# Attention with routed rows on one core: wider table elements, an early block, and a reordered start and end

## The chip, the cores and the metric

The kernel runs on one NeuronCore of a Trainium2 chip. The metric is device time in microseconds (us) of one execution. Engines are named as in the profile: PE (TensorE, its weight loads PEld), DVE (VectorE), ACT (ScalarE), POOL (GpSimd) and SP (SyncE, which here only issues DMAs).

## What is computed

Sigmoid attention over 8 batches and 12 heads (448 tokens, head dimension 64), followed by a mixture-of-depths layer on the joined heads (448 rows of 768 per batch): the 128 rows with the highest gate score go through a two-layer MLP, and the result, weighted by the sigmoid of the score, is added to them.

```python
def _attn_ref(q, k, v):                       # 8 x 12 x 448 x 64, float32
    scale = 1.0 / np.sqrt(q.shape[-1])
    scores = scale * np.matmul(q, k.transpose(0, 1, 3, 2)) - np.log(S)
    attn = 1.0 / (1.0 + np.exp(-scores))
    return np.matmul(attn, v)

def _moe_ref(x, w_gate, w1, w2, capacity):    # x 8 x 448 x 768, w1 768 x 1024, capacity 128
    scores = np.einsum('bsd,d->bs', x, w_gate)
    out = x.copy()
    for b in range(B):
        top_idx = np.argpartition(-scores[b], capacity)[:capacity]
        xe = x[b, top_idx]
        h = np.maximum(xe @ w1, 0.0)
        ye = h @ w2
        g = 1.0 / (1.0 + np.exp(-scores[b, top_idx]))
        out[b, top_idx] = x[b, top_idx] + g[:, None] * ye
    return out
```

## The kernel before, in words

**Attention.** The 96 heads make 24 groups of 4 heads ("quads", three to a batch). A step `s` (12 of them) takes two quads, `x` 0 and 1, and goes through 7 slots `n`. A slot (s, n) holds 16 groups of score matmuls (`score`, L344; 32 x 64 tiles of the array, results in the two PSUM tiles `PA`), two sigmoids on ACT (`squash`, L358) and some of the value matmuls (`value`, L373). These lag: values of step s begin in slot (s, 4) and end in slot (s+1, 3), with NF = 3, and gather in the four PSUM banks `PO[x][pr]`. `rounds` gives the order of the value matmuls of a step; for steps in `LATE` (those from the first step with a block on) `first_slots`, `LOW`, `HIGH` and `last_slot` give another one, in which the banks of quad 0 are done earlier than those of quad 1. `join` writes one element into a bank with ACT (L382), which sets PE's later writes to this bank behind what came before; a `split` slot does it for both quads at once.

q and k are turned on DVE in 32 x 32 blocks (`turn`: L326 to L331 for k into a new tile, L318 for q in place, L321 for the first q by halves). Finished banks are taken out by DVE (`take`, L394) into `x_b` and stored in DRAM as rows of `out` (`store`, L411, packets of 128 bytes).

**Routing.** For each batch DVE forms the gate scores (`gate_part`, `gate`, L402 to L435), which go to DRAM (L430) and come back spread over all partitions (`spread`, L442). `rank` (L450, L453) counts for every token how many score higher. `place` (L457) makes an integer rank of it; then four indirect DMAs on POOL (L464, one for each of NC = 4 columns of tokens) write each token's pair (token, score) from `who`, 8 bytes, to the row of a DRAM table that is its rank, and four plain DMAs on POOL (L469) read the first 128 rows back. Each of the four tables holds only its own column's tokens, the rest being zero from `blank`, so that `fetch` (L485) gets the list by adding the four. Then `gather` (L506, indirect, POOL) fetches the chosen rows, 3 KB each. For the last two batches, 6 and 7, no table is used: DVE makes a 0/1 matrix `hot` (L473), and PE multiplies it with `who` (`choose`, L481).

**MLP.** Batches go in pairs through a scheme of seven products for a 2 x 2 block matrix in each layer: `turn_rows` transposes the gathered rows on PE (L524), `first` (L560) and `second` (L624) are the products of both layers, `first_sums` and `second_sums` their combinations on DVE and ACT. For batches 0 to 5 this work is cut into `BLOCKS`, placed in slot (s, 3) of steps 5 to 11, after the scores of that slot; so the block of step s falls between the ends of slots (s, 3) and (s, 4). What is left (batches 6 and 7, and a part of batches 4 and 5's) is done in `rest` after the last slot.

**Order.** Nothing is scheduled by a planner: the program order is the order of each engine and of each DMA queue. Loads of q, k, weights and the stores are issued by SP, the v loads by SP up to step 5 and by ACT after it; all DMAs of the routing but one are issued by POOL. `after(s, n)` says what follows slot (s, n) on DVE, POOL and SP. Two small lists in it matter here: `RANKED`, the slots of the ranking, and `FETCHED`, those of `fetch`:

```python
RANKED = [(3, 1), None, (6, 1), None, (9, 1), None, (11, 6)]
FETCHED = {(4, 1): 0, (5, 6): 1, (6, 5): 2, (8, 4): 3, (9, 5): 4, (11, 3): 5}
```

Tiles of a pool of one buffer take the place of the last tile of that name: `rows_t` holds early loads of k and v and later the turned rows, `hidden` two early sigmoids and later the hidden layer, and `raw_v` the v of a step.

Of the kernel before, what the change touches and what calls it, by code (L numbers as in the profile page):

```python
# [9 lines left out]
F32 = mybir.dt.float32  # L10
# [7 lines left out]
def kernel(  # L18
# [11 lines left out]
    nc = tc.nc  # L30

    B, H, S, Dh = q.shape
# [98 lines left out]
    NA = NU - 2  # L131

    def load_v(s):


        if s >= NS:
            return
        if s in (1, 3):
            t = moe.tile([P, 6 * KH * P], F32, name="rows_t")[:, :4 * NU * Dh]
        else:  # L140
            t = vals.tile([P, 4 * NU * Dh], F32, name="raw_v")
        raw_v[s] = t = t.rearrange("p (h c) -> p h c", h=4)

        def block(x, r, n):
            return bass.AP(tensor=v.tensor,
                           offset=v.offset + (8 * s + 4 * x) * S * Dh + r * Dh,
                           ap=[[TB * Dh, TT], [S * Dh, 4], [1, n * Dh]])
# [114 lines left out]

    who = [const.tile([P, NC, 2], F32, name=f"who{x}") for x in range(2)]
    tables = [dram.tile([(B - 2) * S, 2], F32, name=f"table{c}", bufs=1) for c in range(NC)]
    slots = const.tile([P, CAP], F32, name="slots")
# [5 lines left out]
    def blank(zero):  # L271

        for t in tables:
            nc.sync.dma_start(out=t.rearrange("(b s) x -> b (s x)", s=S)[:, :2 * CAP],
                              in_=zero[:B - 2, :2 * CAP])

# [32 lines left out]
    def turn(which, *quads):  # L309


        for i in quads:
            if i >= NQ:
                return
            t = heads[which, i].rearrange("p (r e d) -> p e r d", e=2, d=TT)
            if which == "q":
                if i:
                    nc.vector.transpose(heads["q", i], heads["q", i])  # L318
                else:
                    for e in range(2):  # L320
                        nc.vector.transpose(t[:, e], t[:, e])  # L321
                continue
            heads["k", i] = kt = head.tile([P, 2, TB, TT], F32, name="kT")
            for e in range(2):
                if i > 1:
                    nc.vector.transpose(kt[:, e], t[:, e].rearrange("p (a n) d -> p n a d", a=2))  # L326
                else:
                    nc.vector.transpose(
                        kt[:, e, :2 * NA],
                        t[:, e, :2 * NA].rearrange("p (a n) d -> p n a d", a=2))  # L330
                    nc.vector.transpose(  # L331
                        kt[:, e, 2 * NA:],
                        t[:, e, 2 * NA:].rearrange("p (a n) d -> p n a d", a=2))

    def score(s, n, e, pr, out):

        for y in range(2):
            x, c, step = chunks(s, n, y)
            r = 2 * column(s, n, y)
            kt = heads["k", 2 * s + x]  # L340
            qt = heads["q", 2 * s + x].rearrange("p (r e t) -> p e r t", e=2, t=TT)
            for h in range(2 * pr, 2 * pr + 2):
                d = slice(h * TT, (h + 1) * TT)
                nc.tensor.matmul(  # L344
                    out[y * Dh:(y + 1) * Dh, h % 2, :S],
                    kt[d, e, r:r + 2].rearrange("d r t -> d (r t)"), qt[d, e],
                    start=(e == 0), stop=(e == 1))
# [30 lines left out]

    def join(x):

        for t in PO[x]:
            nc.scalar.activation(t[Dh:Dh + 1, S:S + 1], bias_s[Dh:Dh + 1], AF.Copy)  # L382

# [33 lines left out]
    def gate(b):  # L417
# [11 lines left out]
        scores = dram.tile([TB, TT], F32, name="scores")  # L429
        nc.gpsimd.dma_start(out=scores, in_=total[:TB])  # L430
        by_token = moe.tile([TT, TT], F32, name="by_token")
# [25 lines left out]
    def place(b):  # L457

        if b < B - 2:
            rank_of = moe.tile([P, NC], I32, name="rank_of")  # L460
# [7 lines left out]
            for c in range(NC):  # L468
                nc.gpsimd.dma_start(out=rows[:CAP, c], in_=tables[c][b * S:b * S + CAP])  # L469
            return  # L470
# [7 lines left out]
    def choose(b, ps):  # L478

        for c in range(NC):  # L480
            nc.tensor.matmul(ps[:CAP, :2], st[b]["hot"][:, c, :CAP], who[b % 2][:, c, :],  # L481
                             start=(c == 0), stop=(c == NC - 1))
        return b, ps

    def fetch(b, ps=None):  # L485
        n = CAP
        idx = moe.tile([P, 1], I32, name="idx", bufs=5)
        got = moe.tile([P, 2], F32, name="got", bufs=5)
        if b < B - 2:
            nc.vector.tensor_reduce(out=got[:n], in_=st[b]["rows"][:n].rearrange("p c x -> p x c"),  # L490
# [59 lines left out]
    def first(p, key, ps):  # L550
        n = CAP
        x = pairs[p]["x"][:, ROWS1[key]]
        if key == 1:
            t = moe.tile([P, 7 * FH * P], F32, name="hidden")
            pairs[p]["h"] = t.rearrange("p (m k n) -> p m k n", m=7, k=FH)
        w = weight(1, key, p)
# [85 lines left out]
    def scatter(b):  # L642
# [7 lines left out]
    BLOCKS = {  # L650
# [28 lines left out]
    def block(s):  # L679

        places = [PO[0][0], PO[0][1], PA[1][:, 0], PA[0][:, 0], PO[1][0], PO[1][1], PO[1][0]]
        for x in range(2):
            takes(s - 1, x)
# [29 lines left out]
    def rounds(s):  # L713


        if s == 0:
            return [(0, 0, 1), (1, 0, 1), (1, 0, 1), (0, 0, 1), (0, 4, 5), (0, 1, 6), (1, 4, 5)]
        same = [(0, 0, 1), (1, 0, 1), (1, 2, 3), (0, 2, 3), (0, 4, 5)]
# [43 lines left out]
    def last_slot(s, n):  # L762
# [13 lines left out]
        squash(s, n, 0, PA[0])  # L776

    def entries(s, i, half):

        if s in LATE:  # L780
# [3 lines left out]
        if s == 0 and i < 4 and (i < 2) == bool(half):  # L784
            u, w = 2, 3
        return (p, u), (p, w)

    def slot(s, n):


        if s == 0 and n < NF + 1:
# [7 lines left out]
            for pr in (1, 0):  # L799
                squash(s, n, pr, psc[pr])  # L800
            return
        vs, i = (s, n - NF - 1) if n > NF else (s - 1, n + NF)
# [3 lines left out]
        if vs in LATE and n == NF:  # L806
            last_slot(s, n)
            return
        if vs not in LATE and split(vs, i):
            one, two, u = rounds(vs)[i]  # L810
# [11 lines left out]
        for half in range(2):  # L822
            pr = 1 - half
            a, b = entries(vs, i, half)
            if s == 0 and n == NF + 1 and half == 0:
                value(vs, half, *a)
                value(vs, half, *b)
                score(s, n, 0, pr, PA[pr])
            else:
                score(s, n, 0, pr, PA[pr])  # L830
                value(vs, half, *a)
                value(vs, half, *b)
            score(s, n, 1, pr, PA[pr])
            if vs == 0 and half == 1 and i in (1, 3):
                join(1 if i == 1 else 0)
            squash(s, n, pr, PA[pr])
# [3 lines left out]
    def rest():  # L840
# [12 lines left out]
        p, b = NP - 2, B - 1  # L853
        turns[0] = 0
        work = [((1, p, 6), first(p, 6, bank()))]
        chosen = choose(b - 1, bank())
        work.append(((1, p, 7), begin((1, p, 7), bank())))
        gates(2 * NS - 1)
        fetch(*chosen)

# [5 lines left out]
        for key in (4, 5):  # L866
            do((1, p, key))
        first_sums(*begin((1, p, 3), bank()), sums_too=(5, 6))
        work = {key: begin((2, p, key), bank()) for key in (2, 1, 4)}
# [37 lines left out]
    def after(s, n):  # L907

        if n == NF and s:
            odd = s in FULL[1::2]  # L910
            if s > 4 and s not in (6, 9):
                load_v(s)
            elif s < 4:
                load_v(s + 1)
            if s in BLOCKS:
                block(s)
            else:
                stores(s, n)
# [51 lines left out]
    def stream():  # L970
# [59 lines left out]
```

## Time and profile before

| | |
|---|---|
| timed, 5 runs: median (lowest to highest) | 461.68 us (458.21 to 464.34) |
| the profiled execution's own time | 454.62 us |
| its span in the profile | 452.8 us |
| L344 score matmuls on PE | 2624 groups, 249.5 us busy |
| L373 value matmuls on PE | 2176 groups from `raw_v`, 200.6 us busy, and 448 from `rows_t`, 41.9 us |
| L358 sigmoids on ACT | 162, 161.2 us busy, 1007 ns each |
| L464 table writes on POOL | 24, 24.8 us busy, 1033 ns each |
| DMA traffic | 114430 packets, 76.88 MB, mean 170 GB/s |

The span is what lies between the first and the last record of the profiled execution, its own time the device time of the same execution. Matmuls overlap in the array, so that the sum of their busy times is more than the span. In a line of a timeline the columns are start, duration, engine, line of the program, operation, result <- operands, shape and count, and in brackets how long the engine was idle before and what ended this. In the view by windows they are the stretch, its length, the busy time (and number of instructions) of PE, PEld, DVE, ACT and POOL, the granted PE clock, the share of the DMA engines that was busy, and GB/s. In the view of waits they are the total, the number and the longest. An end of a slot is read as the end of its second sigmoid in ACT's timeline.

### The profile page before, as it was taken

What the parts mean: (1) busy time and instruction counts of PE and PEld (TensorE: products, weight loads), DVE (VectorE), ACT (ScalarE), POOL (GpSimd) and SP (SyncE); (2) the same over time, 40 slices, a digit from 0 to 9 for tenths busy, and PEclk for the clock granted to TensorE, in tenths of its full rate; (3) what the DMA queues carried; (4) which work ended last, traced back from release to release, by engine and by line L of the source; (5) the groups of instructions that cost most, each with busy time, mean ns of one, the idle gap of its engine ahead of it and who ended that gap; (6) DMA issues with size and microseconds to landing.
All of it is one profiled execution on the core that took longest, in us unless ns stands there. A gap on an engine that the chain in (4) does not pass through costs nothing.

```text
span 452.8 us, 14325 instructions
## 1 busy us (share of the span) xinstructions
PE 439.1 (97%) x6342; PEld 260.4 (57%) x6342; DVE 289.0 (64%) x601; ACT 191.2 (42%) x257; POOL 72.1 (16%) x102
## 2 busy tenths in 40 slices
PE   7999999999989989999999999999999999999995
PEld 3456554445448449456447638646444758769952
DVE  4317277945919945985877656745773688884372
ACT  4766666466554640660552561463245240102000
POOL 7000000510230040020061104010032200001001
PEclk9999999999999999999999999999999999999999
DMA  8885737997545999569848697299842984511001
GB/s 235 245 243 139 260 86 142 212 224 167 183 126 120 223 261 241 143 169 290 249 141 203 214 259 131 90 270 261 260 141 35 211 235 89 116 36 71 1 1 69
DMA packets 114430, 76.88 MB, mean 170 GB/s; under 512 B 91864, under 2 KB 100720, under 8 KB 114368
## 3 DMA queue, kind: packets, MB, share of 16 engines
q1 hardware_dynamic: 107392, 62.49, 53.5%
q0 software_dynamic: 3520, 7.96, 6.3%
q10 hardware_dynamic: 3456, 5.51, 5.1%
q8 instruction: 50, 0.82, 0.8%
q14 instruction: 12, 0.10, 0.1%
HBM read 55.44 MB, written 20.51 MB: 168 GB/s over the span
## 4 chain that ended last, share of the span: by engine, by line
PE 84%; DMA 4%; DVE 3%; ACT 3%; issue 2%; another core or an unknown queue 2%; POOLq 0%; SPq 0%; POOL 0%; DVEq 0%; ACTq 0%
PE a L344 27%; PE o L373 24%; PE o L624 10%; PE o L560 10%; PE a L560 7%; PE a L624 4%; ACT attn L358 3%; DMA qT<-in_q_dram 2%; DMA rep<-scores 1%; PE o L524 1%; DVE qT L318 1%; DMA out_dram<-xe,idx 1%; DVE scr L450 1%; DVE scr L453 0%
## 5 line engine op out<-in xcount | busy, mean ns | idle before, releaser
L344 PE MATMUL a<-qT,kT 32*64 32x448 f32 x2624 | 249.5, 538 | 1.6 <-issue 0.8
L358 ACT ACTIVATE attn<-a,bias_s 128x896 f32<-128x896 f32 x162 | 161.2, 1007 | 100.2 <-PE a L344 74.2
L373 PE MATMUL o<-attn,raw_v 32*64 32x448 f32 x2176 | 200.6, 537 | 0.3 <-issue 0.2
L344 PEld LDWEIGHTS a<-qT,kT 32*64 32x64 f32 x2624 | 95.4, 131 | 93.7 <-ACT attn L358 53.0
L373 PEld LDWEIGHTS o<-attn,raw_v 32*64 32x64 f32 x2176 | 77.0, 131 | 38.4 <-issue 31.4
L394 DVE STREAM_TRANSPOSE x_b<-o 128x448 f32<-128x448 f32 x48 | 28.1, 626 | 68.9 <-PE o L373 52.9
L373 PE MATMUL o<-attn,rows_t 32*64 32x448 f32 x448 | 41.9, 537 | 0.0
L464 POOL DMA_INDIRECT table<-who,rank_of x24 | 24.8, 1033 | 79.0 <-DVE rank_of L461 73.5
L576 ACT ACTIVATE hidden<-hidden 128x512 f32<-128x512 f32 x12 | 7.5, 630 | 66.0 <-DVE hidden L573 66.0
L405 DVE TENSOR_REDUCE gate_p<-scr 128x14 f32<-128x448 f32 x48 | 29.8, 621 | 1.7
L326 DVE STREAM_TRANSPOSE kT<-raw_k 128x448 f32<-128x448 f32 x42 | 24.1, 612 | 10.2 <-DMA raw_k<-in_k_dram 6.9
L402 DVE TENSOR_TENSOR scr<-x_b,wg_b 128x448 f32<-128x448 f32 x48 | 29.4, 613 | 1.0
L573 DVE TENSOR_TENSOR hidden<-o,hidden 128x512 f32<-128x512 f32 x22 | 14.4, 687 | 21.9 <-PE o L560 21.8
L430 POOL DMA_DIRECT2D scores<-total x8 | 4.6, 579 | 137.4 <-DVE by_token L432 137.4
L560 PE MATMUL o<-rows_t,spare 128*128 128x128 f32 x216 | 25.7, 276 | 0.7 <-DVE x_b L394 0.7
L560 PEld LDWEIGHTS o<-rows_t,spare 128*128 128x128 f32 x216 | 24.7, 192 | 2.9 <-DVE x_b L394 2.9
L318 DVE STREAM_TRANSPOSE qT<-qT 128x896 f32<-128x896 f32 x23 | 25.0, 1086 | 2.2 <-DMA qT<-in_q_dram 2.2
L635 DVE SCALAR_TENSOR_TENSOR xe<-o,gate,xe 128x384 f32<-128x384 f32 x32 | 18.2, 612 | 10.6 <-PE o L624 10.4
L450 DVE TENSOR_SCALAR_CACHE_REDUCE scr<-rep,who 128x448 f32<-128x448 f32 (+1 forms) x32 | 21.6, 674 | 5.3 <-DMA rep<-scores 4.3
L624 PE MATMUL o<-spare,hidden 128*128 128x384 f32 x72 | 24.3, 487 | 0.0
L453 DVE SCALAR_TENSOR_TENSOR scr<-rep,who,earlier 128x448 f32<-128x448 f32 (+1 forms) x32 | 21.8, 683 | 1.4
L373 PEld LDWEIGHTS o<-attn,rows_t 32*64 32x64 f32 x448 | 18.1, 131 | 5.6 <-issue 4.1
(105 smaller groups left out, 399.4 us busy)
## 6 DMA issues: line engine op xcount, KB each, us to landing
qT<-in_q_dram SPq DMA_DIRECT2D x24, 448.0 KB
out_dram<-x_b SPq DMA_DIRECT2D x32, 336.0 KB
raw_k<-in_k_dram SPq DMA_DIRECT2D x22, 448.0 KB
spare<-sum SPq DMA_DIRECT2D x18, 384.0 KB
sum<-spare SPq DMA_DIRECT2D x8, 768.0 KB
raw_v<-in_v_dram ACTq DMA_DIRECT2D x24, 224.0 KB
w_sb<-in_moe_w_dram SPq DMA_DIRECT2D x6, 768.0 KB
raw_v<-in_v_dram SPq DMA_DIRECT2D x12, 224.0 KB
```

Of the source, the lines that this page charges most:

```text
L318: nc.vector.transpose(heads["q", i], heads["q", i])
L326: nc.vector.transpose(kt[:, e], t[:, e].rearrange("p (a n) d -> p n a d", a=2))
L344: nc.tensor.matmul(out[y * Dh:(y + 1) * Dh, h % 2, :S], kt[d, e, r:r + 2].rearrange("d r t -> d (r t)"), qt[d, e], start=(e == 0), stop=(e ...
L358: nc.scalar.activation(a, psc[:, :, :S], AF.Sigmoid, bias=bias_s, scale=QK_SCALE)
L373: nc.tensor.matmul(PO[x][pr][j * Dh:(j + 1) * Dh, :S], raw_v[s][rows, 2 * pr + j, at:at + Dh], attn[s, pr, n][rows, j, :], start=((s, x, p ...
L394: nc.vector.transpose(x_tiles[b][:, :, 2 * g + pr, :], PO[x][pr][:, :S].rearrange("p (r t) -> p r t", t=TT))
L402: nc.vector.tensor_tensor(out=tmp, in0=x_tiles[b][:, :, hp, :], in1=wg_b[:, hp:hp + 1, :].to_broadcast([P, TB, TT]), op=ALU.mult)
L405: nc.vector.tensor_reduce(out=gate_parts[b][:, :, hp], in_=tmp, axis=AX.X, op=ALU.add)
L450: nc.vector.tensor_scalar(out=junk[:n], in0=rep[:n], scalar1=own, scalar2=0.0, op0=ALU.is_gt, op1=ALU.add, accum_out=above[:n, c:c + 1])
L464: nc.gpsimd.indirect_dma_start(out=tables[c][:, :], in_=who[b % 2][:n, c], in_offset=None, out_offset=bass.IndirectOffsetOnAxis(ap=rank_of ...
L560: nc.tensor.matmul(ps[:, f, :n], w((t * FH + f) * P, P), x[:, t, :n], start=(t == 0), stop=(t == KH - 1))
L624: nc.tensor.matmul(ps[:n, :DH], h[:, t, :n], w(t * DH, DH), start=(t == 0), stop=(t == FH - 1))
```

## The change

1. Table elements are 16 values (64 bytes) wide, the pair in the first two and zeros behind it; `who`, the tables and `blank` grow with it, reads take the first two values.
2. Batch 6 goes by the table too, so that its `hot` and `choose` go; its `fetch` comes after keys 4 and 5 of `rest`. The scores of the last batch are written by SP, ahead of the stores, and the banks of `rest` begin at another place of their round.
3. v of step 5 is loaded in slot (4, 3), not (5, 3), and into a part of the `hidden` tile.
4. Step 4 has a block with the transposes of batch 0, which leave the block of step 5. So step 4 is in `LATE`.
5. The values of step 0 begin in slot (0, 3), in the order of the list `FIRST`, without a split slot; its `join` is done by DVE.
6. The first two q are turned by halves into new tiles; the matmuls of the warm-up are shorter.
7. The gate parts of step 2 come behind the turns of q and k, and batch 4 is ranked in slot (9, 0).

```diff
+        elif s == min(BLOCKS) + 1:
+            t = hidden(0)[:, 3 * FH * P:3 * FH * P + 4 * NU * Dh]
         else:
             t = vals.tile([P, 4 * NU * Dh], F32, name="raw_v")
...
-    who = [const.tile([P, NC, 2], F32, name=f"who{x}") for x in range(2)]
-    tables = [dram.tile([(B - 2) * S, 2], F32, name=f"table{c}", bufs=1) for c in range(NC)]
+    WIDE = 16
+    who = [const.tile([P, NC, WIDE], F32, name=f"who{x}") for x in range(2)]
+    tables = [dram.tile([(B - 1) * S, WIDE], F32, name=f"table{c}", bufs=1) for c in range(NC)]
...
-            nc.sync.dma_start(out=t.rearrange("(b s) x -> b (s x)", s=S)[:, :2 * CAP],
-                              in_=zero[:B - 2, :2 * CAP])
+            rows = t.rearrange("(b s) x -> b (s x)", s=S)[:, :WIDE * CAP]
+            nc.sync.dma_start(out=rows.rearrange("b (q y) -> b q y", y=NC * P),
+                              in_=zero[:(B - 1) * WIDE * CAP // (NC * P)])
...
-                if i:
+                if i > 1:
                     nc.vector.transpose(heads["q", i], heads["q", i])
-                else:
-                    for e in range(2):
-                        nc.vector.transpose(t[:, e], t[:, e])
+                    continue
+                heads["q", i] = qt = head.tile([P, TB * Dh], F32, name="qT")
+                qt = qt.rearrange("p (e r t) -> p e r t", e=2, t=TT)
+                for e in range(2):
+                    nc.vector.transpose(qt[:, e], t[:, e])
...
-    def join(x):
+    def join(x, by_vector=False):
         for t in PO[x]:
+            if by_vector:
+                nc.vector.memset(t[Dh:Dh + 1, S:S + 1], 0.0)
+                continue
             nc.scalar.activation(t[Dh:Dh + 1, S:S + 1], bias_s[Dh:Dh + 1], AF.Copy)
...
-        nc.gpsimd.dma_start(out=scores, in_=total[:TB])
+        (nc.sync if b == B - 1 else nc.gpsimd).dma_start(out=scores, in_=total[:TB])
...
     def place(b):
-        if b < B - 2:
+        if b < B - 1:
...
-                nc.gpsimd.dma_start(out=rows[:CAP, c], in_=tables[c][b * S:b * S + CAP])
+                nc.gpsimd.dma_start(out=rows[:CAP, c], in_=tables[c][b * S:b * S + CAP, :2])
...
     BLOCKS = {
-        5: [("t", 0), (1, 0, 1), (1, 0, 2)],
+        4: [("t", 0)],
+        5: [(1, 0, 1), (1, 0, 2)],
...
+        if s == NF + 1:
+            places = [PA[1][:, 0], PO[0][0]]
...
+    FIRST = [[(0, (0,)), (1, (0, 1)), (1, (2, 3)), (0, (2, 3)), (0, (1, 4)), (0, (5, 6)),
+              (1, (4, 5)), (1, (6,))],
+             [(0, (2,)), (1, (2, 3)), (1, (0, 1)), (0, (0, 1)), (0, (3, 4)), (0, (5, 6)),
+              (1, (4, 5)), (1, (6,))]]
...
+            if n == NF:
+                for half in range(2):
+                    for a in entries(0, -1, half):
+                        value(0, half, *a)
+                for x in range(2):
+                    join(x, by_vector=True)
             return
...
-        if vs not in LATE and split(vs, i):
+        if vs and vs not in LATE and split(vs, i):
...
-            if vs == 0 and half == 1 and i in (1, 3):
-                join(1 if i == 1 else 0)
+            if vs == 0 and half == 1 and i in (0, 2):
+                join(0 if i else 1, by_vector=True)
...
-        turns[0] = 0
+        turns[0] = 5
         work = [((1, p, 6), first(p, 6, bank()))]
-        chosen = choose(b - 1, bank())
         work.append(((1, p, 7), begin((1, p, 7), bank())))
         gates(2 * NS - 1)
-        fetch(*chosen)
...
         for key in (4, 5):
             do((1, p, key))
+        fetch(b - 1)
...
-            if s > 4 and s not in (6, 9):
+            if s > 5 and s not in (6, 9):
                 load_v(s)
-            elif s < 4:
+            elif s < 5:
                 load_v(s + 1)
...
-            if s == 2:
-                gates(2 * s - 2)
...
-            if s not in FULL[::2]:
+            if s not in FULL[::2] or s not in BLOCKS:
                 gates(2 * s - 2)
...
-    RANKED = [(3, 1), None, (6, 1), None, (9, 1), None, (11, 6)]
+    RANKED = [(3, 1), None, (6, 1), None, (9, 0), None, (11, 6)]
...
-        for _ in range(3):
-            nc.tensor.matmul(outs[1][:, 0], zero[:, :P], zero, start=True, stop=True)
+        for cols in (4 * P, 4 * P, 2 * P):
+            nc.tensor.matmul(outs[1][:, 0, :cols], zero[:, :P], zero[:, :cols],
+                             start=True, stop=True)
```

More of the change, by code (lines that the diff above doesn't have):

```diff
@@ L131, with hidden @@
     NA = NU - 2
+    hiddens = {}
+    def hidden(p):
+        if p not in hiddens:
+            hiddens[p] = moe.tile([P, 7 * FH * P], F32, name="hidden")
+        return hiddens[p]
     def load_v(s):
@@ L340, in score @@
             kt = heads["k", 2 * s + x]
-            qt = heads["q", 2 * s + x].rearrange("p (r e t) -> p e r t", e=2, t=TT)
+            qt = heads["q", 2 * s + x].rearrange(
+                "p (r e t) -> p e r t" if s else "p (e r t) -> p e r t", e=2, t=TT)
             for h in range(2 * pr, 2 * pr + 2):
@@ L480, in choose @@
         for c in range(NC):
-            nc.tensor.matmul(ps[:CAP, :2], st[b]["hot"][:, c, :CAP], who[b % 2][:, c, :],
+            nc.tensor.matmul(ps[:CAP, :2], st[b]["hot"][:, c, :CAP], who[b % 2][:, c, :2],
                              start=(c == 0), stop=(c == NC - 1))
@@ L488, in fetch @@
         got = moe.tile([P, 2], F32, name="got", bufs=5)
-        if b < B - 2:
+        if b < B - 1:
             nc.vector.tensor_reduce(out=got[:n], in_=st[b]["rows"][:n].rearrange("p c x -> p x c"),
@@ L553, in first @@
         if key == 1:
-            t = moe.tile([P, 7 * FH * P], F32, name="hidden")
-            pairs[p]["h"] = t.rearrange("p (m k n) -> p m k n", m=7, k=FH)
+            pairs[p]["h"] = hidden(p).rearrange("p (m k n) -> p m k n", m=7, k=FH)
         w = weight(1, key, p)
@@ L713, in rounds @@
     def rounds(s):
-        if s == 0:
-            return [(0, 0, 1), (1, 0, 1), (1, 0, 1), (0, 0, 1), (0, 4, 5), (0, 1, 6), (1, 4, 5)]
         same = [(0, 0, 1), (1, 0, 1), (1, 2, 3), (0, 2, 3), (0, 4, 5)]
@@ L776, in last_slot @@
         squash(s, n, 0, PA[0])
+    FIRST = [[(0, (0,)), (1, (0, 1)), (1, (2, 3)), (0, (2, 3)), (0, (1, 4)), (0, (5, 6)),
+              (1, (4, 5)), (1, (6,))],
+             [(0, (2,)), (1, (2, 3)), (1, (0, 1)), (0, (0, 1)), (0, (3, 4)), (0, (5, 6)),
+              (1, (4, 5)), (1, (6,))]]
     def entries(s, i, half):
+        if s == 0:
+            p, some = FIRST[half][i + 1]
+            return [(p, n) for n in some]
         if s in LATE:
@@ L783, in entries @@
         p, u, w = rounds(s)[i]
-        if s == 0 and i < 4 and (i < 2) == bool(half):
-            u, w = 2, 3
         return (p, u), (p, w)
@@ L823, in slot @@
             pr = 1 - half
-            a, b = entries(vs, i, half)
-            if s == 0 and n == NF + 1 and half == 0:
+            score(s, n, 0, pr, PA[pr])
+            for a in entries(vs, i, half):
                 value(vs, half, *a)
[L827 to L832, printed above, removed]
             score(s, n, 1, pr, PA[pr])
-            if vs == 0 and half == 1 and i in (1, 3):
-                join(1 if i == 1 else 0)
+            if vs == 0 and half == 1 and i in (0, 2):
+                join(0 if i else 1, by_vector=True)
             squash(s, n, pr, PA[pr])
```

## The prediction, made before the changed kernel had run

> **What bounds the kernel now.** I read the page first, then the waits, the chain of waits, and the timelines of single engines around each wait. The page's first part and its timeline of the granted clock:
>
> ```profile
> span 452.8 us, 14325 instructions
> PE 439.1 (97%) x6342; PEld 260.4 (57%) x6342; DVE 289.0 (64%) x601; ACT 191.2 (42%) x257; POOL 72.1 (16%) x102
> PEclk9999999999999999999999999999999999999999
> ```
>
> TensorE counts as busy nearly throughout and its clock is never held back, so a gain must be sought where PE is "busy" without getting on. The waits of ScalarE show such a place:
>
> ```profile
> ACT attn L358 <- remote: 15.4, 6, 4.1
> ```
>
> Six times the sigmoid waits long for a score that the profile lays to nobody on the chip's engines. ScalarE's timeline around one of them (start, duration, idle time before it with releaser):
>
> ```profile
> 120.90 1.01 ACT L358 ACTIVATE attn<-a,bias_s 128x896 f32<-128x896 f32 x1 [0.56 <-PE a L344]
> 124.27 1.01 ACT L358 ACTIVATE attn<-a,bias_s 128x896 f32<-128x896 f32 x1 [2.36 <-remote]
> 127.34 1.01 ACT L358 ACTIVATE attn<-a,bias_s 128x896 f32<-128x896 f32 x1 [2.07 <-remote]
> 129.00 1.01 ACT L358 ACTIVATE attn<-a,bias_s 128x896 f32<-128x896 f32 x1 [0.65 <-PE a L344]
> ```
>
> A slot ends with its second sigmoid. The slot before ends at 121.91 (120.90 + 1.01), this one at 128.35: 6.44 us. The view by windows sets it beside its predecessor:
>
> ```profile
> 118.90:121.91 3.01, 3.01 (x72) 1.27 (x64) 2.87 (x9) 2.01 (x2) 0.47 (x1) 1.00 0.76 281
> 121.91:128.35 6.44, 6.08 (x72) 2.36 (x64) 2.76 (x5) 2.02 (x3) 5.15 (x7) 1.00 0.38 91
> ```
>
> The same 72 matmul groups take twice as long, at clock 1.00 and with the DMAs half idle. Only POOL is busier; its timeline says with what:
>
> ```profile
> 121.44 1.13 POOL L464 DMA_INDIRECT table<-who,rank_of  x1 [21.25 <-DVE rank_of L461]
> 122.88 0.96 POOL L464 DMA_INDIRECT table<-who,rank_of  x1 [0.30 <-issue]
> 124.14 0.92 POOL L464 DMA_INDIRECT table<-who,rank_of  x1 [0.30 <-issue]
> 125.37 0.91 POOL L464 DMA_INDIRECT table<-who,rank_of  x1 [0.30 <-issue]
> ```
>
> Those are the scatters of 8-byte (token, score) elements. They start at 81.78, 121.44, 160.65, 228.49, 271.29 and 335.00 for batches 0 to 5, and the chain shows long pieces of "another core or an unknown queue" beside four of them:
>
> ```profile
> 82.42 2.30 another core or an unknown queue
> ...
> 229.76 2.30 another core or an unknown queue
> ...
> 336.60 4.12 another core or an unknown queue
> ```
>
> **The change, part by part.** The sum is made against the profiled execution (454.62 around a span of 452.8); the five timed runs have their median at 461.68, 7.06 higher, and I put the difference on that.
>
> *Elements of 64 bytes.* Excess per batch, from slot ends (a plain slot takes 3.02): batch 0, slots (3,3) and (3,4), 5.54 + 4.90 against 3.60 + 3.29 in steps 1, 2 and 4: 3.55. Batch 1: 6.44 - 3.02 = 3.42. Batch 2: 23.31 for (6,3) and (6,4), against 20.61 for the like pair of step 9: 2.70. Batch 3: 4.30 + 3.45 - 6.04 = 1.71. Batch 4, beside a routed block: 0. Batch 5: 6.13 + 3.45 - 6.04 = 3.54. Sum 14.9; the waits say 15.4. The operation alone is not to blame: the row gathers of L506 are the same POOL operation with 3 KB elements, and the slots around them lose 0 to 0.7. Nor are small packets: the row stores at 106 to 110 us put out over 1000 packets of 128 bytes per us, and their slots stay at 3.02. What is special is the 8-byte element, and 64 is far nearer to 128 than 8 is. I take -14.0 (about 0.15 left per batch, as the gathers leave); ends 0 and -15.4, a loss being a rival below. The four blanking DMAs on SP at 29 us carry eight times as much, 0.23 MB, 0.9 us at the 245 GB/s of that slice; the loads behind them are wanted a step later: 0, to +0.9.
>
> Rule and row differ here. The row: 128-byte stores leave TensorE alone. The Trainium skill, "DMA: Bandwidth & Descriptors", section Specifications, says that a transfer under 512 bytes makes the DMA engine read, modify and write. By that rule 64 bytes are no better than 8, this part would be worth 0, and the whole forecast would stand near 459 (461.68 - 3.5 + 0.5).
>
> *Batch 6 by the table.* It adds four L464 (0.97 each) and four L469 (0.55) on POOL at about 371 to 378, a time in which POOL did nothing (0.00 in that window); behind them only gather 6 queues, whose rows are transposed past 405. It drops hot on DVE (0.69). If its scatters stall the value matmuls like the others it costs up to 3.5; I take +0.5, ends 0 and +3.5.
>
> *End part.* Choose(6) leaves PE, and the new bank order takes the first matmuls of key 6 off a bank that DVE still empties:
>
> ```profile
> 375.86 2.94 PE L560 MATMUL o<-rows_t,spare 128*128 128x128 f32 x24 [0.70 <-DVE x_b L394]
> 378.64 0.95 PE L481 MATMUL o<-who,hot 128*128 128x2 f32 x8
> ```
>
> That is 0.70, and 0.81 from 378.64 to 379.45, when the next matmul starts: -1.5. Against it, scores(7) now goes by SP, ahead of the stores. In the run of before SP issued two stores at 377.43, while the gate parts ran, and had the queue clear for the broadcast:
>
> ```profile
> 386.11 0.33 SPq L442 DMA_DIRECT2D rep<-scores  x1
> ```
>
> Now these stores wait on SP for the total (384.2) and the broadcast queues behind them: their packets took 378.5 to 384.2, say 5.5 us from 386, so rep lands near 393.4 and the ranking, which began at 392.60, starts 0.8 later. The second choose is then ready near 400.2 to 401, and PE, 1.5 ahead of before, gets there at 399.1: it waits 1 to 2. I take 1.2: net -0.3; ends -1.5 and +1.0. After it the end is bound by matmuls up to 443, unchanged.
>
> *Start.* PE waits for the second q:
>
> ```profile
> 10.27 1.76 PE L344 MATMUL p<-qT,kT 32*64 32x448 f32 x32 [0.99 <-DVE qT L318]
> ```
>
> By halves (1.11 in all, 0.56 for the first) it can go 0.5 earlier. Values of step 0 begin a slot earlier, into time when PE waits for sigmoids, and the bank-joining writes leave ScalarE, where `21.28 0.26 ACT L382` delays a sigmoid. Slots (0,4) to (1,3) take 3.53, 3.28, 3.36, 3.15, 3.31, 3.07 and 3.56, that is 2.1 above seven plain ones. With the first values of step 0 already done in (0,3), those seven hold less, and (0,3) more. I take -2.2 for the part; ends -2.8 and -1.0 (the halves and the joins alone). The memsets are behind DVE's turns, which in step 0 have waits of 0.4 to 0.8 to spare. The shorter warm-up is worth 0: the first score waits for DVE.
>
> *A block in step 4, v of step 5.* Before, slots (4,2) to (4,5) took 3.13 + 3.62 + 3.27 + 3.02 = 13.04, and slot (5,4), with the block, 10.66: 23.70. The block starts with the transposes:
>
> ```profile
> 134.86 1.03 PE L524 MATMUL o<-iden,xe 128*128 128x128 f32 x6 [0.86 <-issue]
> ```
>
> They take 1.03, and PE stands from 133.5 to 134.86 (1.34) since all four banks are taken out at once from 134.11. Blocks 7, 8 and 10 follow a step in the later order, and PE goes straight from L344 into their first matmul. So block 5 after a step in that order should lose both: 10.66 - 1.03 - 1.34 = 8.3. Step 4 gets the transposes, the first three into a bank of scores, so some 0.3 of wait: 13.04 + 1.03 + 0.3 = 14.4 (the rows, gathered at 99.17 and landed by 104, are wanted at 107.5). 14.4 + 8.3 - 23.7 = -1.0; ends -2.0 (the odd 0.6 of slot (4,3) goes too) and +0.5 (both waits stay). v of step 5 was issued at 134.09 and used from 141.9; with a shorter block that would be close, so its load a step earlier hides it. It goes past the k load on SP, 0.23 MB or 0.9 us, wanted two slots later: 0, to +0.9.
>
> *With one answer.* Ranking 4 a slot earlier on DVE still waits for its broadcast (the chain has it landing at 265.0): 0, to +3.4 if its scatters leave the cover of block 9. Gate parts of step 2 behind the q turns: DVE work beside PE, 0.
>
> Sum: -14.0 + 0.5 - 0.3 - 2.2 - 1.0 = -17.0, so 437.6 in the profiled execution and 444.7 on the median.
>
> **The rivals.** (1) The stall belongs to four indirect writes in a row, of whatever size of element. For it: in batch 2 the matmuls slow before its first packet (164.5). Against: with batches 0, 1, 3 and 5 the slowing comes within 0.3 of the first packets. Then the tables give 0, batch 6 adds 14.9/6 = 2.5, and the small parts stay at -2.2 - 1.0 - 0.3 = -3.5: 2.5 - 3.5 = -1.0, so 460.7. (2) Half remains, each element still being a write of its own: -7.5 + 1.2 - 3.5 = -9.8, 451.9. (3) Slower: the stall grows with the bytes written (28 KB in place of 3.5 per batch). For it: scatters land late, 4 to 7 us after issue. It decides from the point where the mean stall of seven batches passes (14.9 + 3.5)/7 = 2.63 (3.3 for 1%); doubled to 5.0 it gives 35 - 18.4 = +16.6, so 478.
>
> **How the numbers follow.** Likeliest case 0.62, (2) 0.15, (1) 0.17, (3) 0.06. The likeliest reaches from -15.4 - 2.8 - 2.0 - 1.5 = -21.7 (440.0) to 453 (-12 of the tables, +2.5 for batch 6, -1.0, +0.5 and +1.0 for the small parts: -9). Five runs spread 3 to each side of their median, which takes the low end to 437; the high end, 461, takes in half of (1). Faster by over 1% (below 457): 0.62 + 0.15 = 0.77; within 1%, about what a measurement of this kernel can tell from no change: 0.17; slower: 0.06.
>
> **What would show it.** Tables: no wait of L358 on "remote", slots with scatters at 3.0 to 3.3. If these waits stay, (1) holds; if longer, (3). Start: slot (1,3) ends near 36.7, not 39.02. Block: slot (5,4) near 8.3. End: a wait of about 1 on PE ahead of the second choose. I am wrong if the matmuls stall beside 64-byte scatters as beside 8-byte ones.

## The result, and the profile after

The changed kernel takes 463.46 us (median of 40 runs, 459.13 to 469.68) against 460.54 for the kernel before (77 runs): a ratio of 1.0089, 95% interval 1.0068 to 1.0109, or 4.1 us slower. Its profiled execution took 463.38 us around a span of 461.1. One thing must be known to read the runs below: the kernel before takes 455 to 467 us in all sets of runs but one, in which it took 437.9 us (25 runs, 436.41 to 440.81) and the traced kernels with as many indirect DMAs show no stall; another set on that same chip gave 459.57 again, so ratios are taken only within a set, and what decides between the two is not known.

The page after, its first part and the granted clock:

```profile
span 461.1 us, 14316 instructions
PE 444.9 (96%) x6334; PEld 260.6 (57%) x6334; DVE 288.3 (63%) x609; ACT 190.6 (41%) x249; POOL 78.0 (17%) x109
PEclk9999999899989999999999999999998999999998
```

PE has 8 matmuls fewer and is busy 5.8 us longer, and the clock, before at full speed throughout, dips in four slices. The waits of ACT after:

```profile
ACT attn L373 <- remote: 20.6, 5, 6.8
```

The waits that were to go have grown from 15.4 to 20.6. Around batch 1's scatters, ACT's timeline and POOL's:

```profile
125.38 1.01 ACT L373 ACTIVATE attn<-a,bias_s 128x896 f32<-128x896 f32 x1 [0.82 <-PE a L359]
130.53 1.01 ACT L373 ACTIVATE attn<-a,bias_s 128x896 f32<-128x896 f32 x1 [4.14 <-remote]
132.02 1.01 ACT L373 ACTIVATE attn<-a,bias_s 128x896 f32<-128x896 f32 x1 [0.48 <-PE a L359]
```

```profile
124.80 1.13 POOL L482 DMA_INDIRECT table<-who,rank_of  x1 [21.18 <-DVE rank_of L479]
126.23 0.98 POOL L482 DMA_INDIRECT table<-who,rank_of  x1 [0.30 <-issue]
127.51 0.92 POOL L482 DMA_INDIRECT table<-who,rank_of  x1 [0.30 <-issue]
128.74 0.91 POOL L482 DMA_INDIRECT table<-who,rank_of  x1 [0.30 <-issue]
```

Slot (5,1) ends at 133.03 and took 6.64, with 64-byte elements as with 8-byte ones (6.44). The window of this slot adds one thing (columns as in front: length, busy times, clock, DMA share, GB/s):

```profile
126.39:133.03 6.64, 6.47 (x50) 2.07 (x56) 1.70 (x3) 2.02 (x3) 4.35 (x6) 0.83 0.59 195
```

PE's clock is 0.83 here, and 0.86 over the next slot, which takes 4.25 instead of 3.12. The loss of clock does not come with every stall: the kernel before kept 1.00 in this slot through a stall as long, and 0.89, with 0.79 after it, in another execution (e5). Where the two traces part, by ends of slots (after less before, summed up; then what the stretch adds):

| up to the end of | after - before | this stretch | what lies in it |
|---|---|---|---|
| (1,3) | 38.64 - 39.02 = -0.4 | -0.4 | the new start |
| (3,2) | 79.75 - 80.28 = -0.5 | -0.1 | |
| (3,5) | 95.93 - 93.73 = +2.2 | +2.7 | ranking of batch 0 late |
| (5,0) | 126.39 - 121.91 = +4.5 | +2.3 | block in step 4 |
| (5,4) | 149.90 - 145.25 = +4.7 | +0.2 | batch 1's stall longer, block 5 shorter |
| (8,6) | 265.30 - 260.69 = +4.6 | 0.0 | |
| (9,4) | 295.62 - 290.36 = +5.3 | +0.7 | slot (9,0) +0.6, scatters of batch 4 |
| (11,6) | 376.44 - 369.94 = +6.5 | +1.2 | batch 5's stall longer |
| the end | 461.1 - 452.8 = +8.3 | +1.8 | scatters of batch 6 |

These are one execution of each; the timed difference is half of it. The ranking first. The scores of batch 0 now leave DVE behind the turns, 3 us later; POOL's timeline shows them, and the broadcast, 5.9 later than before (68.04):

```profile
68.67 0.79 POOL L448 DMA_DIRECT2D scores<-total  x1 [59.80 <-DVE by_token L450]
73.92 0.60 POOL L460 DMA_DIRECT2D rep<-scores  x1 [4.46 <-DMA scores<-total]
```

DVE's timeline shows what it does to the queue behind, and PE's where it ends:

```profile
79.32 0.68 DVE L468 TENSOR_SCALAR_CACHE_REDUCE scr<-rep,who 128x448 f32<-128x448 f32 x1 [6.20 <-DMA rep<-scores]
...
85.46 2.24 DVE L412 STREAM_TRANSPOSE x_b<-o 128x448 f32<-128x448 f32 x4
```

```profile
86.17 1.54 PE L388 MATMUL o<-attn,rows_t 32*64 32x448 f32 x6 [3.24 <-DVE x_b L412]
86.74 1.03 PE L359 MATMUL a<-qT,kT 32*64 32x448 f32 x4
```

DVE stands 6.2 us before the first count of the ranking, and the takes of step 3, queued behind all of it, come at 85.46 instead of 81.40. PE, which must not write into these banks before they are out, waits 3.24. Its next matmuls last about 950 ns where 534 is usual, and (3,4), in which the scatters of batch 0 now fall as well, runs at a clock of 0.82 by its window. The Trainium skill, "TensorE: Matmul & The Clock Gate", Part 1, says that the clock follows how busy PE has lately been; the row agrees.

### The profile page after: what moved, and what is told of

Same layout as the page of the kernel before. It is cut to its first block, busy times and chain, and to the rows that moved or that the text cites. A ratio compares the mean times of both kernels' runs of the same rounds, so it can differ in the third digit from the quotient of the medians.

```text
span 461.1 us, 14316 instructions
## 1 busy us (share of the span) xinstructions
PE 444.9 (96%) x6334; PEld 260.6 (57%) x6334; DVE 288.3 (63%) x609; ACT 190.6 (41%) x249; POOL 78.0 (17%) x109
## 5 line engine op out<-in xcount | busy, mean ns | idle before, releaser
L359 PE MATMUL a<-qT,kT 32*64 32x448 f32 x2624 | 253.7, 546 | 1.0 <-ACT attn L373 0.4
L388 PE MATMUL o<-attn,raw_v 32*64 32x448 f32 x1952 | 186.4, 542 | 0.3 <-issue 0.2
L359 PEld LDWEIGHTS a<-qT,kT 32*64 32x64 f32 x2624 | 97.0, 133 | 94.2 <-ACT attn L373 52.5
L388 PEld LDWEIGHTS o<-attn,raw_v 32*64 32x64 f32 x1952 | 71.5, 133 | 37.0 <-issue 30.8
L412 DVE STREAM_TRANSPOSE x_b<-o 128x448 f32<-128x448 f32 x48 | 27.7, 624 | 72.9 <-PE o L388 56.9
L388 PE MATMUL o<-attn,rows_t 32*64 32x448 f32 x448 | 43.6, 560 | 3.2 <-DVE x_b L412 3.2
L482 POOL DMA_INDIRECT table<-who,rank_of x28 | 28.9, 1030 | 89.4 <-DVE rank_of L479 83.0
L388 PE MATMUL o<-attn,hidden 32*64 32x448 f32 x224 | 23.1, 537 | 1.1 <-DVE hidden L590 0.7
L330 DVE STREAM_TRANSPOSE qT<-qT 128x896 f32<-128x896 f32 x22 | 23.7, 1078 | 0.0
L577 PE MATMUL o<-rows_t,spare 128*128 128x128 f32 x192 | 23.0, 276 | 0.0
L577 PEld LDWEIGHTS o<-rows_t,spare 128*128 128x128 f32 x192 | 22.1, 192 | 1.4 <-DVE x_b L412 1.4
```

The source lines that it names most:

```text
L359: nc.tensor.matmul(out[y * Dh:(y + 1) * Dh, h % 2, :S], kt[d, e, r:r + 2].rearrange("d r t -> d (r t)"), qt[d, e], start=(e == 0), stop=(e ...
L388: nc.tensor.matmul(PO[x][pr][j * Dh:(j + 1) * Dh, :S], raw_v[s][rows, 2 * pr + j, at:at + Dh], attn[s, pr, n][rows, j, :], start=((s, x, p ...
L412: nc.vector.transpose(x_tiles[b][:, :, 2 * g + pr, :], PO[x][pr][:, :S].rearrange("p (r t) -> p r t", t=TT))
L482: nc.gpsimd.indirect_dma_start(out=tables[c][:, :], in_=who[b % 2][:n, c], in_offset=None, out_offset=bass.IndirectOffsetOnAxis(ap=rank_of ...
L577: nc.tensor.matmul(ps[:, f, :n], w((t * FH + f) * P, P), x[:, t, :n], start=(t == 0), stop=(t == KH - 1))
```

## The experiments

**Whether the size of the elements matters, alone.** e8 is the kernel before with `WIDE = 16` and nothing else.

> The kernel before with only the table elements 64 bytes wide, batches 0 to 5 as before. Prediction on record: 14 us faster. Theory A2: size of element is of no account; within 1.5 us of before, stalls or none. Rival: eight times the bytes cost: 2 to 6 us slower.

Measured: 1.0016 (0.9977 to 1.0054). The waits and the window of slot (5,1):

```profile
ACT attn L359 <- remote: 13.4, 5, 4.1
```

```profile
121.94:128.49 6.55, 6.17 (x72) 2.10 (x64) 2.83 (x5) 2.01 (x3) 5.24 (x7) 1.00 0.41 129
```

The 14 us are 0.7 slower, within the uncertainty of none, and the stall is there at 6.55 us.

**What holds PE: four kernels in surroundings without stalls.** In e1 the scatters are left out; in e2 to e4 they are exchanged, for plain writes, for indirect reads, and for indirect writes of 512 bytes. So that all else runs alike, `fetch` takes its rows from a counter (`ramp`): batches 0 to 5 route their first 128 tokens.

```diff
-        ... tensor_scalar(out=idx[:n], in0=got[:n, 0:1], ...
+        ... tensor_scalar(out=idx[:n], in0=(ramp if b < B - 2 else got)[:n, 0:1], ...
 e1:
-                nc.gpsimd.indirect_dma_start(out=tables[c][:, :], in_=who[b % 2][:n, c], ...
 e2:
+                nc.gpsimd.dma_start(out=spots[c][:n], in_=who[b % 2][:n, c])
 e3:
+                nc.gpsimd.indirect_dma_start(out=junk[:n, c], in_=pairs_of_q, in_offset=...
 e4:
+                nc.gpsimd.indirect_dma_start(out=tables[c][:, :], in_=iden[:n], ...   # rows of 128
```

> The kernel before, with the 24 table scatters (L464) left out. So that the rest runs as before, the routed rows are the first 128 tokens of batches 0 to 5 instead of the chosen ones. Theory A (every indirect DMA on POOL, whatever it moves, holds back PE's instructions from about 1.7 us after POOL starts it, for 0.6 to 0.9 us): the six waits on 'remote' go, 12 to 15 us faster. Theory B (small writes to DRAM hold PE back): the same. Third, if the stalls exist only in a profiled execution: the waits go, but the timed runs stay within 2 us of before.

> The kernel before, with each of the 24 indirect scatters replaced by a plain DMA on POOL that writes the same 8-byte elements of the same partitions to a DRAM table in order (routing as in the run without scatters). Theory A: no indirect DMA, no stall, 12 to 15 us faster. Theory B: the small writes stay, so the stalls stay: within 3 us of before.

> The kernel before, with each scatter replaced by an indirect read with the same indices, 8 bytes per partition from DRAM into SBUF (routing as in the run without scatters). Theory A: 24 indirect DMAs as before, the stalls stay: within 3 us of before. Theory B: nothing small is written to DRAM, so the stalls go: 12 to 15 us faster.

> The kernel before, with table elements of 512 bytes (128 values from a constant tile; routing as in the run without scatters). Theory A: stalls as before, within 3 us. Theory B: elements this large should cost no more than the gathers of rows: 12 to 15 us faster.

This is the set in which the kernel before took 437.9. e1: 1.0002 (0.9973 to 1.0031); e3: 1.0026 (0.9995 to 1.0058); e4: 1.0033 (1.0010 to 1.0056). Nothing was there to be taken away, so neither theory was tested; what can be read is that without stalls the scatters cost nothing measurable (e1), and elements of 512 bytes in their place 0.3% (e4). e2 took 454.38 (448.27 to 461.4, 4 runs, no ratio): slots (3,2), (5,0), (6,3), (9,2) and (11,0) at 4.4 to 5.2. These are not slots of its writes, which need no rank and so went out 4 us or more earlier; in (3,2) and (9,2) the DMA engines were busy throughout (a share of 1.45 and 1.20) and moved 59 and 38 GB/s. Why plain 8-byte writes come with that stays open.

**The kernel before and the changed kernel again, and the late ranking undone.** e5 is the kernel before, e6 the changed one; in e7 the gate parts of step 2 go back ahead of the turns:

```diff
                 stores(s, n)
+            if s == 2:
+                gates(2 * s - 2)
             turn("q", 2 * s + 2)
...
-            if s not in FULL[::2] or s not in BLOCKS:
+            if s not in FULL[::2]:
```

> The kernel before, unchanged, for a profile of it on the chip of these runs. In the runs with the scatters taken out or changed the kernel before took 437.9 us, 23 less than in the first runs, and the changed forms the same. Theory A2 (the stalls beside indirect DMAs depend on the chip or its surroundings): where it takes about 438, its profile has no wait of ACT on 'remote' and its slots with scatters take 3.0 to 3.6; where it takes about 460, they are there. Rival: the 23 us lie elsewhere (a clock held back, slower transfers), and the stalls are in the profile whatever the time.

> The changed kernel, unchanged. Theory A2 with what the two traces show of the other parts (gate parts of step 2 later: +2.2; block in step 4: +0.7; start: -0.5; end: +1.8, of which part is the stall of batch 6): where before takes 438, +2 to +4 us; where it takes 460, +3 to +5. Rival, that the change lost only through stalls: within 1 us of before where before takes 438.

> The changed kernel with the gate parts of step 2 put back ahead of the turns of q and k. Theory: they write the scores of batch 0, whose broadcast then came 4 us late and with it the ranking and the takes of step 3 behind it on DVE, for which PE waited 3.2 us; so 2 to 3 us faster than the changed kernel, and slot (3,4) back at 3.2 to 5. Rival: DVE's delay is made up by waits that PE has anyway: within 0.7 us of the changed kernel.

e5 took 456.54 in its one run; it has the stalls ("remote" 13.4 in 5 waits, slot (5,1) 6.51). e6: 1.0090 (1.0047 to 1.0132), as before. e7: 1.0046 (1.0009 to 1.0083), so putting the gate parts back is worth about 0.44%, 2.0 us, some 1.7 either way; the wait of 3.24 of PE for L412 is gone, and (3,3) and (3,4) take 10.41 together, at full clock, against 13.06 after and 10.44 before. That is one of three parts that made the change slower than no change.

**The block in step 4 alone, and the old end.** e11 is the kernel before with `4: [("t", 0)]` split off, its `places` and the early v; e12 is e7 with the old end (batch 6 by `hot` and `choose`, scores of batch 7 on POOL, `turns[0] = 0`).

> The kernel before, with only the block of step 4 and the early load of v of step 5. By the two traces: +1.1 (slots (4,4) and (4,5) +2.5, slot (5,0) +0.35; given back -0.5, -0.15 and -1.1). The prediction on record had -1.0. So 0.5 to 2 us slower by the traces, 0.5 to 1.5 faster by the prediction.

> The changed kernel with the gate parts of step 2 early and the end part as before (batch 6 by the 0/1 matrix, scores of batch 7 on POOL, first banks as before). In the traces the changed end is 1.6 to 1.8 longer (its four scatters stall the value matmuls): so where before takes about 460, 1 to 2.5 us faster than the changed kernel with early gate parts, which took 1.0046 of before; where it takes 438, within 1 us of it.

e11: 1.0022 (0.9979 to 1.0064), +1.0 us, on the side of the traces but within its own uncertainty. e12: 0.9974 (0.9938 to 1.0009), against 1.0046 for e7 in another set: the new end costs some 3 us, 2 either way; the two traces show 1.8. PE's timeline after shows how:

```profile
375.50 8.46 PE L388 MATMUL o<-attn,raw_v 32*64 32x448 f32 x111
384.14 0.97 PE L388 MATMUL o<-attn,raw_v 32*64 32x448 f32 x3 [0.18 <-issue]
385.04 2.94 PE L577 MATMUL a<-rows_t,spare 128*128 128x128 f32 x24
```

The batch's four scatters start at 378.47, and the last value matmuls trickle until 385. From the end of slot (11,6) to the matmuls of key 7 it is 11.38 us after and 9.51 before: +1.9, though the 0.70 for the bank and the 0.81 of choose are saved. So the stall is put at 3.4.

**The scatters taken away where there are stalls.** e9 gives the routing of batches 1 to 5 to DVE and PE, inside the blocks:

```diff
-        if b < B - 2:
+        if b < 1:
             rank_of = ...
...
+            if s in CHOSEN and item is BLOCKS[s][0]:
+                fetch(*choose(CHOSEN[s], PA[1][:, 1]))
+    CHOSEN = {5: 1, 6: 2, 8: 3, 9: 4, 11: 5}
```

> The kernel before, with batches 1 to 5 routed without the table: DVE makes the 0/1 matrix, and PE multiplies it with the pairs inside the next routed block (choose, 0.81 us each by its row in the profile), so that 20 of the 24 table scatters are gone. Theory A2: where before takes about 460, the stalls of these batches (3.4 + 2.7 + 1.7 + 0.8 + 3.5 = 12.1) go and 5 x 0.8 of PE come: 7 to 9 us faster; where it takes about 438, 3 to 5 us slower. Rival: the stalls are not caused by the scatters but fall beside them (the ranking on DVE, the loads of that slot): 3 to 5 us slower on any chip.

> The run before it, and the start of the changed kernel (values of step 0 from slot (0,3), joins on DVE, q by halves). The traces give the start -0.9 where the prediction on record had -2.2: so 0.5 to 1.5 us faster than with choose on PE alone; 1.8 to 2.8 if the prediction's size was right.

e9: 1.0102 (1.0043 to 1.0161), e10: 1.0103 (1.0038 to 1.0168): slower, as the rival had it, and still the slots are as the theory has them. All slots that lost their scatters are at 3.0 to 3.1, while batch 0, which kept them, still stalls; the blocks are longer, block 5 by 7.6 us, for a reason that PE's timeline of e9 names:

```profile
134.02 0.95 PE L481 MATMUL a<-who,hot 128*128 128x2 f32 x8
140.13 2.26 PE L560 MATMUL a<-rows_t,w_sb 128*128 128x128 f32 x9 [5.16 <-DVE got L493]
```

The next product went into the same tile as the list, and DVE's copy of the list stood behind the takes and gate parts of 7 us. A total would have refuted the right theory; the slots did not. e13 moves choose ahead of the last product of a block, in a bank that nothing soon uses; e14 adds the start of the changed kernel:

```diff
-            if s in CHOSEN and item is BLOCKS[s][0]:
-                fetch(*choose(CHOSEN[s], PA[1][:, 1]))
+            if s in CHOSEN and item is BLOCKS[s][0 if s == NS - 1 else -2]:
+                fetch(*choose(CHOSEN[s], PO[0][1] if s in (6, 9) else PO[1][1]))
```

> As the run with choose on PE, but choose stands ahead of the last product of its block (in the last block behind the first one), in a bank that nothing soon uses, so that PE does not wait for DVE's copy of the list, for which it waited 11.7 us there. Theory A2 (indirect DMAs hold PE back, in surroundings in which before takes about 460): slots (5,1), (6,2), (6,3), (8,1), (9,3) and (11,1) at 3.0 to 3.1 and blocks no more than 1.5 longer than before; 6 to 10 us faster where before takes 460, 3 to 5 slower where it takes 438. Rival: the list on PE costs what the scatters cost: within 2 us of before.

> The run before it with the start of the changed kernel. From the traces 1 us faster than it, from the prediction on record 2.2.

e13: 0.9786 (0.9710 to 0.9862), e14: 0.9757 (0.9691 to 0.9824): about 10 and 11 us faster than the kernel before, and both faster than either kernel of this study. The waits and slot (5,1) of e13:

```profile
ACT attn L358 <- remote: 4.4, 2, 2.3
```

```profile
122.35:125.37 3.02, 3.02 (x72) 1.13 (x64) 2.92 (x6) 2.02 (x3) 0.00 (x0) 1.00 0.04 8
```

What is left of "remote" is batch 0, which still scatters. So the stalls come with the table's way of routing; e13 drops the reads of the table too and moves the gathers into the blocks, but e18 below keeps both and has no stall, which leaves the scatters. What the start is worth these two do not tell: e14's ratio is 0.3% lower than e13's, but its median (449.05) is higher (447.82).

**Operation, direction, size, elements, number.** e15 and e16 repeat e3 and e4 in surroundings with stalls; in e17 each scatter has 32 partitions instead of 128 and 96; in e18 there is one scatter for each batch, not four (routing by the counter in all four).

```diff
 e17:
-            for c, n in enumerate(HELD):
+            for c, n in enumerate((32,) * NC):
 e18:
-            for c, n in enumerate(HELD):
+            for c, n in enumerate(HELD[:1]):
```

> The same kernel as in the earlier run with indirect reads of 8 bytes instead of the scatters (routing of batches 0 to 5 by the first 128 tokens), for a profile in which before takes about 460. Theory A2: slots (5,1), (6,3) and (11,1) take 5.5 to 7 as before. Theory B (small writes): 3.0 to 3.2.

> The same kernel as in the earlier run with elements of 512 bytes (routing as there), for a profile in which before takes about 460. Theory A2: slots (5,1), (6,3) and (11,1) take 5.5 to 7 as before. Theory B (size of the elements written): 3.0 to 3.3.

> The kernel before with each of the 24 scatters cut to 32 partitions, a quarter of the elements (routing of batches 0 to 5 by the first 128 tokens). If the hold on PE goes by the operation: slot (5,1) takes 5.5 to 7 as before, where before takes about 460. If it goes by the elements: 3.4 to 4.2.

> The kernel before with one scatter of 128 partitions for each batch instead of four (routing as in the other run). If each indirect DMA adds its hold: slot (5,1) takes 3.2 to 3.9, like slots beside the single gathers of rows, where before takes about 460; if the first one makes most of it: over 5.

One run each, beside 461.13 for the kernel before (11 runs): 464.47, 470.91, 466.46, and 441.39 with one scatter. Slot (5,1) in e15, in e16, in e17 and in e18, from the windows:

```profile
123.21:129.88 6.67, 6.25 (x65) 2.34 (x61) 2.83 (x5) 2.01 (x2) 5.74 (x8) 0.89 0.35 114
```

```profile
130.16:136.84 6.68, 6.26 (x72) 2.15 (x64) 2.83 (x5) 2.02 (x3) 5.23 (x7) 1.00 0.48 153
```

```profile
121.69:128.32 6.63, 6.37 (x66) 2.14 (x61) 2.79 (x5) 2.02 (x3) 4.95 (x7) 0.93 0.42 128
```

```profile
120.06:123.08 3.02, 2.96 (x64) 1.30 (x64) 1.64 (x3) 2.02 (x3) 0.93 (x2) 1.00 0.21 33
```

Reads, 512 bytes and a quarter of the elements: the same stall. One operation instead of four: slot (5,0), in which it starts, 3.35, slot (5,1) 3.02, no wait on "remote" in the whole run. e17 and e18 move the same 128 elements for a batch, in four operations and in one. So the hold goes by the operation, and four at a distance of 1.3 us make much more (3.6 us) than four times one (0.3).

A rival remains to be closed: e18 is one run, and it could have met the surroundings in which nothing stalls. A gather that all these kernels issue at the end of slot (10,0) tells them apart. Slot (10,2) behind it in e18, and in e1 of the set without stalls:

```profile
293.73:297.18 3.45, 3.45 (x88) 1.67 (x76) 0.00 (x0) 2.02 (x2) 0.52 (x1) 1.00 1.10 174
291.08:294.08 3.00, 3.00 (x74) 1.54 (x68) 0.00 (x0) 2.01 (x2) 0.56 (x1) 1.00 1.24 190
```

Slots (10,1) and (10,2) together take 6.7 in the kernel before and in e18, and 6.0 in e1, e3 and e4, as in e9, which gathers elsewhere. So e18 ran where indirect DMAs do hold PE, and had no stall of the kind that four make.

## Why the prediction was wrong, point by point

- **The tables (-14.0; measured 0).** The step that failed: "What is special is the 8-byte element, and 64 is far nearer to 128 than 8 is." The stalls were seen rightly, and so were their place and nearly their price (14.9; with and without scatters, by the slots of before and of e1: 3.6 + 3.5 + 3.7 + 1.7 + 1.1 + 3.6 = 17.2). Their cause was not: I let "the row gathers of L506 are the same POOL operation" acquit the operation, and compared one gather with four scatters in a row. The comparison changed two things, the bytes and the number; e8 and e16 show that it is not the bytes, e17 and e18 that it is the number. The clue was on record under rival (1): in batch 2 the matmuls slow before the first packet. It was weakened there by a reading that does not hold for batch 5, where PE has slowed by 337.2 and the first packet starts at 337.7. In batches 0 to 3 and 5 PE slows some 1.6 to 2.2 us after POOL starts the first operation, whatever the packets do (batch 4's fall beside a block, where it can't be read). The row set against small packets was misread as well: at 106 to 110 us the stores put out 880 packets per us, and their slots take 3.62 and 3.27, not 3.02. Slots (3,6) and (9,1), with 1260 and 965 such packets per us, do take 3.0, so the stores stay acquitted.
- **The rule weighed against the row.** By the rule of the Trainium skill ("DMA: Bandwidth & Descriptors", Specifications) 64 bytes are no better than 8, and the total it gave, near 459, was nearer than mine, by luck: its reason isn't borne out here, since at 512 bytes the stall is the same (6.68).
- **Gate parts of step 2 (0; measured +2.0).** "DVE work beside PE, 0" looked at the moved work and not at what starts behind it: the scores, their way through DRAM, the ranking, and in DVE's queue the takes for which PE waits (3.24).
- **Batch 6 and the end (+0.5 - 0.3; in the traces +1.8).** The end of the range that was set for "stall like the others", +3.5, is what came (3.4). The broadcast did land late (DVE waits 0.83 for it), but PE was as late, so the wait ahead of the second choose did not come.
- **The block (-1.0; e11 +1.0).** Block 5 went straight into its products, as worked out, but took 9.54, not 8.3. Of the 1.2 too much one row shows 0.7, and the rest stays open. Putting v of step 5 into the tile of the hidden layer tied the value matmuls to the sums that write this tile:

```profile
146.35 0.59 PE L388 MATMUL o<-attn,hidden 32*64 32x448 f32 x2 [0.69 <-DVE hidden L590]
```

  And "other order, the same matmuls" has a price: slot (4,5) takes 3.76, as the like slots of steps 5 to 10 do (3.53 to 3.76), where step 4 had 3.02; slot (5,0) takes 3.38. e11's +1.0 lies within its own uncertainty of nothing, but the slots of the two traces add up to the same +1.1.
- **The start (-2.2; -0.9, or up to -1.6).** Slots (0,4) to (1,3) sum to 22.3 instead of 23.3 (e7: the same). The joins and the split are gone, but the work of slot (0,3) moved the wait to (0,4), which went from 3.53 to 3.84. And q by halves gained nothing in the profiled run, PE waiting 1.54 for the second q, whose load was late (DVE waits 0.99 for it, 0.43 before):

```profile
10.82 1.76 PE L359 MATMUL p<-qT,kT 32*64 32x448 f32 x32 [1.54 <-DVE qT L335]
```

  In e7 PE does not wait for it. Over all traces slot (1,3) ends at 37.5 to 38.8 in the six with the new start (median 37.9) and at 38.8 to 42.5 in the fourteen with the old one (median 39.6), so the gain up to there is nearer to 1.6. Timed, it is lost in the noise (e10 against e9, e14 against e13).

Sum of the parts as measured: 0.7 (e8) + 2.0 + 1.8 + 1.0 - 0.9 = +4.6; the whole was +4.1. Each part is uncertain by 1 to 2 us, so that the agreement is partly luck. Rival (1), at 0.17, had the cause nearly right, though not only writes do it; its total, -1.0, had the end about right (2.5 - 0.3) and missed the gate parts and the block.

## What to carry to other kernels

When a stall is laid to one property of an operation, look for the row that differs in that property alone; a row that differs in two acquits nothing. Price a moved step by what starts when it ends: its transfers, what waits for them, and what stands in that engine's queue behind the wait. And read an experiment by its slots as well as by its total: e9 was slower and spoke for the theory, and, with its waits for the list repaired, choose on PE made the fastest kernels of the study.

## What the runs showed of the hardware that was not expected

Indirect DMAs of POOL hold back TensorE's instructions, in all sets of runs here but one. From some 1.6 to 2.2 us after the start of the first, four in a row cost 3.5 to 3.7 us in four batches of six and 1.1 to 1.7 in the others; one costs 0 to 0.7. Four do so whether they read or write (e15), 8, 64 or 512 bytes (before, e8, e16), 128 or 32 elements each (e17). Through what they do it is open, and so is why one set of runs showed nothing of it (437.9 us for the kernel before); nor was it tried to set the four scatters further apart in time, which e18 suggests. One candidate the trace of the kernel before speaks against: the DMA view of 120 to 129 us lists packets of the queues "hardware_dynamic" and "software_dynamic" alone and none of "instruction", so that PE, held back in 121.91 to 128.35, was not waiting for a transfer on that queue that landed then. A TensorE so starved, or made to wait 3.2 us, comes back in some executions at a granted clock of 0.74 to 0.93 over a slot or two, with matmuls of about 950 ns instead of 534 (after, e5, e15, e17); in others the clock stays at 1.00 through the same stall (before, e8, e16).
